# Another PSUM pool for the state product, attention stages one slot sooner, and a higher rank for some VectorE operations

## The chip, the cores and the metric

The kernel runs on one core of a Trainium2 chip. The metric is the time of one execution on the device in microseconds (us), from the first to the last instruction with what lies around them; less is better. The engines are TensorE (PE in the rows, with its weight loads as PEld), VectorE (DVE), ScalarE (ACT), GpSimd (POOL) and the DMA queues, most of them issued by SyncE (SP). Each engine works through its own instructions in order and waits on semaphores for the others.

## The reference

Linear attention with a decaying state, then two feed-forward layers on its output. There are 4 batches, 8 heads, 768 tokens and 48 features per head; the first layer is 384 to 2048 to 384, the second 384 to 1024 to 384.

```python
for t in range(S):                      # attention, per batch and head
    cur = einsum('bhd,bhe->bhde', u * k_t, v_t)
    y_t = einsum('bhd,bhde->bhe', r_t, state + cur)
    state = w_t[..., None] * state + einsum('bhd,bhe->bhde', k_t, v_t)
x = y as tokens x (heads * features)    # 3072 x 384
h = x @ w_in
x = (h * clip(h + 3, 0, 6) / 6) @ w_out
h = x @ w_in2
h = h * softmax(h);  h = layernorm(h) * g_ln
out = h @ w_out2
```

## The kernel before

**Attention.** The sequence is cut into 6 groups of 128 tokens; with 4 batches that makes 24 tiles, numbered i = 4 * group + batch. For a tile the decay of the state is a product along the tokens, so that the tile becomes matmuls. Its stages are `stw` (GpSimd clips w into wc), `st0` (TensorE transposes wc to wt and r to rt; VectorE scans wt backward into q, L500, four scans, takes a reciprocal and scans wt forward into e, L506, four scans; then e = rt * e, L510), `st1` (TensorE transposes k to kt; VectorE q = kt * q, L524; GpSimd z = r * k, then z * u, L526 and L527), `st2` (a transpose ktp of q, read by ScalarE; VectorE sums z into d, L561; TensorE pa = e * q in two halves; GpSimd makes the diagonal block am from d, L572, for each half; VectorE copies the strictly causal part of pa over it, L576) and `st3` (TensorE kv, the product that goes into the state, L585, and yt, the output, L600 and L607; VectorE adds kv to the decayed state, L626; ScalarE rounds yt to xh and VectorE makes the rest xl, L639). Tiles from 10 on get their transposes in another way; L626, L639 and st2 are the same there.

**First layer.** A group's four tiles give 512 tokens, and its weights are used in 16 slots n: `ffn_in(n)` makes h in 9 matmuls (high and low parts of x and of the weights), ScalarE, VectorE (L662, t) and ScalarE again make gh from it, GpSimd makes the rest gl, and `ffn_out(n - 2)` adds 9 matmuls into y. The slots of group 0 run while the attention of tiles 4 to 8 does. The weights of the first slots also come in at that time, packed, and are decoded by ScalarE (L63, L71) and VectorE: L66, L50, L53 and L72 on 128 x 768 elements, once each for a slot, from buffers `raw` that are loaded again when L53 has read them.

**PSUM.** `ps_a` has three banks, which wt, rt, kt, ktp, the two halves pa, kv and yt take in turn; a tile that takes a bank waits until the last reader of the one before is done. `ps_h` has two, for h. y has three of its own. kv of the tiles up to 8 is in `ps_a`, later in `ps_h`:

```python
kv = ps_tile("kv") if i < JOIN - 1 else ps_h.tile([P, HP, P], F32, tag="h", name="kv")
```

**Order.** A table gives each stage of each tile a slot, 4 slots for a tile, and `back` moves a stage ahead of the slot (negative) or behind it:

```python
back = 2 if s == NS - 1 else s - 3 if i < JOIN else s - 5
sched.setdefault(4 * (i - B) + back, []).append((i, s))
```

On TensorE, VectorE, ScalarE and GpSimd a scheduler then sets the order by priority, which follows the program's order unless something raises it; SyncE keeps the program's order.

Of the kernel before, what the change touches and what calls it, by code (L numbers as in the profile page):

```python
# [8 lines left out]
F32 = mybir.dt.float32  # L9
# [4 lines left out]
ALU = mybir.AluOpType  # L14
# [4 lines left out]
P = 128  # L19
# [259 lines left out]
def fast_path(  # L279
# [14 lines left out]
    nc = tc.nc  # L294
# [4 lines left out]
    C = P  # L299
# [157 lines left out]
    def stw(i):  # L457
# [25 lines left out]
            out=junk, in_=a["w"][:, :, 0:D], func=ACTF.Relu, bias=b_hi, accum_out=chk[:, 3 * i + 1:3 * i + 2]  # L483
        )

    def st0(i):
        a = at[i]
        g = i // B
        if i < LATE:
            wt = ps_in(i, "wt", "y0")  # L490
            trans(wt, a["wc"])
            rt = ps_in(i, "rt", "y1")
            trans(rt, a["r"])
        else:
            wt, rt = flip("w"), flip("r")
        q = atp.tile([P, HP, C + 1], F32, tag="q", name="q")
        e = atp.tile([P, HP, C], F32, tag="e", name="e")
        nc.gpsimd.memset(q[0:DP, :, C:C + 1], 1.0)
        for hp in range(HP):
            nc.vector.tensor_tensor_scan(  # L500
                out=q[0:DP, hp, 0:C][:, ::-1], data0=wt[0:DP, hp, :][:, ::-1], data1=ones[0:DP, :],
                initial=1.0, op0=ALU.mult, op1=ALU.mult,
            )
        nc.vector.reciprocal(out=e[0:DP, :, 0], in_=q[0:DP, :, 0])
        for hp in range(HP):
            nc.vector.tensor_tensor_scan(  # L506
                out=e[0:DP, hp, 1:C], data0=wt[0:DP, hp, 0:C - 1], data1=ones[0:DP, 0:C - 1],
                initial=e[0:DP, hp, 0:1], op0=ALU.mult, op1=ALU.mult,
            )
        nc.vector.tensor_tensor(out=e[0:DP], in0=rt[0:DP], in1=e[0:DP], op=ALU.mult)  # L510
        a.update(q=q, e=e)

    def st1(i):
        a = at[i]
        g, b = divmod(i, B)
        q = a["q"]
        if i < LATE:
            kt = ps_in(i, "kt", "y2")
            trans(kt, a["k"])
        else:  # L520
            kt = flip("k")
        if 0 < g and i < JOIN:
            state_in(i)
        nc.vector.tensor_tensor(out=q[0:DP, :, 1:C + 1], in0=kt[0:DP], in1=q[0:DP, :, 1:C + 1], op=ALU.mult)  # L524
        z = a["r"][:, :, 0:D]
        nc.gpsimd.tensor_tensor(out=z, in0=z, in1=a["k"][:, :, 0:D], op=ALU.mult)  # L526
        nc.gpsimd.tensor_tensor(out=z, in0=z, in1=u_bc, op=ALU.mult)  # L527
        a["z"] = z
# [17 lines left out]
    def st2(i):  # L546
        a = at[i]
        g = i // B
        kq = a["q"][:, :, 1:C + 1]
        rr = a["e"]  # L550
        if g < NG - 1:
            ktp = ps_tile("ktp")
            for hp in range(HP):
                nc.tensor.transpose(out=ktp[:, hp, 0:DP], in_=kq[0:DP, hp, :], identity=ident[0:DP, 0:DP])
            ktok = atp.tile([P, HP, DP], F32, tag="ktok", name="ktok")
            nc.scalar.activation(out=ktok, in_=ktp[:, :, 0:DP], func=ACTF.Copy)
            a["ktok"] = ktok
        a["am"] = []
        pas = [ps_tile("pa0"), ps_tile("pa1")]
        d = atp.tile([P, H], F32, tag="d", name="d")  # L560
        nc.vector.tensor_reduce(out=d, in_=a["z"], axis=AX.X, op=ALU.add)  # L561
        for j in range(HP):
            for hh, pa in enumerate(pas):
                o = 64 * hh
                nc.tensor.matmul(
                    out=pa[:, j, :], lhsT=kq[o:o + D, j, :], rhs=rr[o:o + D, j, :], start=True, stop=True
                )
        dv = d.rearrange("p (j hh) -> p hh j", hh=2)
        for hh, pa in enumerate(pas):
            am = atp.tile([P, 4, C], F32, tag="am", name="am")  # L570
            a["am"].append(am)
            nc.gpsimd.tensor_tensor(  # L572
                out=am, in0=ident.unsqueeze(1).to_broadcast([P, HP, C]),
                in1=dv[:, hh, :].unsqueeze(2).to_broadcast([P, HP, C]), op=ALU.mult,
            )
            nc.vector.copy_predicated(am, causal.unsqueeze(1).to_broadcast([P, HP, C]), pa)  # L576

    def st3(i):
        a = at[i]
        g, b = divmod(i, B)  # L580
        if g < NG - 1:
            kv = ps_tile("kv") if i < JOIN - 1 else ps_h.tile([P, HP, P], F32, tag="h", name="kv")
            for h in range(H):
                o = 64 * (h % 2)
                nc.tensor.matmul(  # L585
                    out=kv[o:o + D, h // 2, 0:D], lhsT=a["ktok"][:, h // 2, o:o + D], rhs=a["v"][:, h, :],
                    start=True, stop=True, skip_group_check=True,
                )
# [31 lines left out]
        if g < NG - 1:  # L620
            for j in range(2):
                o, f = 64 * j, D * j
                dst = s_st[b][o:o + D, :, f:f + D]
                src = kv[o:o + D, :, 0:D]
                if g > 0:
                    nc.vector.tensor_tensor(out=dst, in0=src, in1=a["sp"][o:o + D, :, f:f + D], op=ALU.add)  # L626
                else:
                    nc.scalar.activation(out=dst, in_=src, func=ACTF.Copy)
        at.pop(i)
# [6 lines left out]
        sl = slice(b * C, (b + 1) * C)  # L636
        xf = y[:, 0:KD, :]
        nc.scalar.activation(out=xh[:, :, sl], in_=xf, func=ACTF.Copy, accum_out=chk[:, 3 * i + 2:3 * i + 3])
        nc.vector.tensor_tensor(out=xl[:, :, sl], in0=xf, in1=xh[:, :, sl].bitcast(F32), op=ALU.subtract)  # L639

    stages = [stw, st0, st1, st2, st3]

# [160 lines left out]
    sched = {}  # L803
    for i in range(B, NTILE):
        for s in range(NS):
            back = 2 if s == NS - 1 else s - 3 if i < JOIN else s - 5
            sched.setdefault(4 * (i - B) + back, []).append((i, s))
    for n in sorted(q for q in sched if q < 0):
        for i, s in sched[n]:
# [5 lines left out]
    for n in range(NSLOT + LAG):  # L815
        if n < NSLOT:
            ffn_in(n)
        for i, s in sorted(sched.get(n, []), key=lambda x: (x[0] - 2 * (x[0] >= JOIN and x[1] == 3), x[1])):
            stages[s](i)
            if s == NS - 1 and JOIN <= i + 1 < NTILE:  # L820
                state_in(i + 1)
            if s == 3:
                load_to(i + 3)
            if s == (0 if i + 1 == LATE else 2) and LATE <= i + 1 < NTILE:
                load_late(i + 1)
        if n >= LAG:
            ffn_out(n - LAG)
        if n + LD < M1:
            w1_b(n + LD)
        if n + LD + 1 < M1:  # L830
            w1_a(n + LD + 1)
        if n + LD + 3 < M1:
            w1_load(n + LD + 3)
        if n == M1:
            dec_st.close()
            late_open()
        if n == NA:
            row = range_a()
            right.close()
            w2_open()  # L840
            w2_load(0)
            w2_load(1)
        j = n - NA
        if 1 <= j <= 2 * M2:
            w2_b(j - 1)
        if 0 <= j < 2 * M2:
            w2_a(j)
        if 1 <= j <= 2 * M2 - 2:
            w2_load(j + 1)
# [115 lines left out]
```

## Time and profile before

| | |
|---|---|
| three runs | 781.13 us median (779.6, 781.13, 781.53) |
| the profiled execution | 780.79 us |
| its span, first to last instruction | 779.1 us |
| mean granted clock of TensorE | 0.976 |
| TensorE busy | 736.6 us (95%) |
| VectorE busy | 531.6 us (68%) |
| ScalarE busy | 333.6 us (43%) |
| GpSimd busy | 262.0 us (34%) |

The profiled execution lasts 1.7 us longer than its span, and lies within the three runs. A share of busy time is a mean over stages that differ: the stretch in which the weights of the first layer are decoded, up to about 143 us, is read by itself. A granted clock of 1 is TensorE's upper level, 2.4 GHz, and 0.5 is 1.2 GHz.

### The profile page before, as it was taken

To read this page: it belongs to the slowest core of one execution; us is meant where nothing else is said; L and a number is where in the kernel's file an instruction comes from. 1 tells how busy PE (TensorE), PEld (TensorE's weight loads), DVE (VectorE), ACT (ScalarE), POOL (GpSimd) and SP (SyncE) were. 2 spreads that over 40 slices of the span, in tenths; PEclk is the share of its full clock that TensorE was granted. 3 is DMA by queue.
4 is the path that set the end of the run, shared out by engine and by line. 5 is a ranking of instruction groups with operands and counts; after the bars stand their busy time and mean duration, and the time that the engine had idled before them with its cause. 6 is when DMAs were issued, how large, how long until landed. Compare 5 with 4: busy or idle time off the path is not lost. (4 is left out here: it accounts for less than half of the span.)

```text
span 779.1 us, 13589 instructions
## 1 busy us (share of the span) xinstructions
PE 736.6 (95%) x5084; PEld 621.3 (80%) x5084; DVE 531.6 (68%) x1010; ACT 333.6 (43%) x647; POOL 262.0 (34%) x355
## 2 busy tenths in 40 slices
PE   6669798999999999999999999999999999999996
PEld 4547676888888888888888887877889999999996
DVE  6989889667677777777778856886565555555552
ACT  3455555334444334433344335654444344333442
POOL 5566647642333233333233211232222222222200
PEclk8889997999999999999999999999999999999999
DMA  9785653514345333433334003440111111111001
GB/s 172 176 167 138 163 131 97 108 41 86 84 85 126 84 84 85 125 85 85 85 89 120 1 1 104 145 133 26 61 42 42 51 41 41 48 45 42 31 20 36
DMA packets 139435, 64.79 MB, mean 83 GB/s; under 512 B 90848, under 2 KB 133984, under 8 KB 139360
## 3 DMA queue, kind: packets, MB, share of 16 engines
q1 hardware_dynamic: 136768, 59.11, 32.2%
q10 hardware_dynamic: 2592, 4.72, 1.6%
q8 instruction: 42, 0.69, 0.4%
q14 instruction: 33, 0.27, 0.1%
HBM read 54.37 MB, written 9.44 MB: 82 GB/s over the span
## 5 line engine op out<-in xcount | busy, mean ns | idle before, releaser
L677 PE MATMUL y<-gh,w_h 128*128 128x512 f32 x288 | 116.7, 405 | 1.0 <-ACT ye L683 1.0
L657 PE MATMUL h<-xh,w_h 128*128 128x512 f32 x288 | 113.0, 393 | 3.0 <-DVE t L662 2.9
L677 PE MATMUL y<-gl,w_h 128*128 128x512 f32 x288 | 114.0, 396 | 0.0
L677 PE MATMUL y<-gh,w_l 128*128 128x512 f32 x288 | 113.4, 394 | 0.0
L657 PE MATMUL h<-xl,w_h 128*128 128x512 f32 x288 | 112.8, 392 | 0.0
L657 PE MATMUL h<-xh,w_l 128*128 128x512 f32 x288 | 112.5, 391 | 0.0
L661 ACT ACTIVATE t<-h,cols 128x512 f32<-128x512 f32 x96 | 65.3, 681 | 104.9 <-PE h L657 101.8
L663 ACT ACTIVATE gh<-t 128x512 fp32r<-128x512 f32 x96 | 60.5, 630 | 103.7 <-DVE t L662 103.5
L662 DVE SCALAR_TENSOR_TENSOR t<-t,h 128x512 f32<-128x512 f32 x96 | 65.4, 681 | 41.2 <-ACT t L661 41.0
L665 DVE TENSOR_TENSOR gl<-t,gh 128x512 fp32r<-128x512 f32 x80 | 66.8, 835 | 36.0 <-ACT gh L663 35.0
L78 DVE TENSOR_REDUCE nm<-h 128x1 f32<-128x1024 f32 x24 | 29.4, 1226 | 61.5 <-PE h L872 61.4
L899 PE MATMUL po<-w_oh,qh 128*128 128x384 f32 x192 | 67.1, 350 | 0.3 <-ACT qh L888 0.3
L657 PEld LDWEIGHTS h<-xh,w_h 128*128 128x128 f32 x288 | 54.4, 189 | 16.0 <-DVE t L662 4.2
L677 PEld LDWEIGHTS y<-gh,w_h 128*128 128x128 f32 x288 | 54.7, 190 | 15.5 <-issue 3.2
L899 PE MATMUL po<-w_oh,ql 128*128 128x384 f32 x192 | 64.7, 337 | 0.1
L899 PE MATMUL po<-w_ol,qh 128*128 128x384 f32 x192 | 64.8, 337 | 0.0
L677 PEld LDWEIGHTS y<-gh,w_l 128*128 128x128 f32 x288 | 54.9, 191 | 11.8
L677 PEld LDWEIGHTS y<-gl,w_h 128*128 128x128 f32 x288 | 55.0, 191 | 11.0 <-DVE gl L665 0.6
L657 PEld LDWEIGHTS h<-xh,w_l 128*128 128x128 f32 x288 | 54.4, 189 | 11.3
L657 PEld LDWEIGHTS h<-xl,w_h 128*128 128x128 f32 x288 | 54.4, 189 | 11.2
L888 ACT ACTIVATE qh<-pt 128x512 fp32r<-128x512 f32 x48 | 26.1, 597 | 78.3 <-PE pt L886 78.3
L872 PE MATMUL h<-w_ih,yl 128*128 128x512 f32 x144 | 56.4, 391 | 0.0
(123 smaller groups left out, 1478.7 us busy)
## 6 DMA issues: line engine op xcount, KB each, us to landing
raw<-in_moe_w_out_dram SPq DMA_DIRECT2D x24, 384.0 KB, 5.9
raw<-in_moe_w_in_dram SPq DMA_DIRECT2D x48, 128.0 KB
r<-in_r_dram SPq DMA_DIRECT2D x24, 192.0 KB
k<-in_k_dram SPq DMA_DIRECT2D x24, 192.0 KB, 3.7
v<-in_v_dram SPq DMA_DIRECT2D x24, 192.0 KB, 4.0
y1d<-ye ACTq DMA_DIRECT2D x18, 256.0 KB, 2.3
y<-y1d SPq DMA_DIRECT2D x24, 192.0 KB, 2.8
out_dram<-os SPq DMA_DIRECT2D x24, 192.0 KB, 1.9
```

What stands on the lines that cost most here:

```text
L78: nc.vector.tensor_reduce(out=nm, in_=h, axis=AX.X, op=ALU.max, negate=True)
L657: nc.tensor.matmul(out=h, lhsT=a, rhs=b, start=(j == 0), stop=(j == len(ops) - 1))
L661: nc.scalar.activation(out=t, in_=h, func=ACTF.Relu, bias=three)
L662: nc.vector.scalar_tensor_tensor(out=t, in0=t, scalar=6.0, in1=h, op0=ALU.min, op1=ALU.mult)
L663: nc.scalar.activation(out=gh, in_=t, func=ACTF.Copy)
L665: eng.tensor_tensor(out=gl, in0=t, in1=gh.bitcast(F32), op=ALU.subtract)
L677: nc.tensor.matmul(out=y_ps[g][c], lhsT=a, rhs=b, start=(m == 0 and j == 0), stop=(m == M1 - 1 and j == 2))
L872: nc.tensor.matmul(out=h[:, fs], lhsT=a[:, c, :], rhs=b_[:, c, fs], start=(j == 0), stop=(j == len(ops) - 1))
L888: nc.scalar.activation(out=qh[:, ms, :], in_=pt, func=ACTF.Copy)
L899: nc.tensor.matmul(out=po, lhsT=x[:, m, :], rhs=y[:, m, :], start=(n == 0), stop=(n == 3 * M2 - 1))
```

## The change

It adds and removes no instruction. The state product kv of the tiles from 4 on goes into the h pair, so that `ps_a` has seven takers for a tile instead of eight. For tiles 5 to 9 `stw`, `st0` and `st1` come one slot sooner (`back` of -4, -3, -2 instead of -3, -2, -1); `st2` and `st3` stay. The VectorE operations of L510, L524, L576, L626 and L639 of tiles 4 to 9 get a raised priority. One load of tile 10 is issued with another stage, in the same slot.

```diff
--- before.py
+++ after.py
@@ -483,6 +483,9 @@
             out=junk, in_=a["w"][:, :, 0:D], func=ACTF.Relu, bias=b_hi, accum_out=chk[:, 3 * i + 1:3 * i + 2]
         )
 
+    def early(i):
+        return tc.high_priority() if B <= i < JOIN else ExitStack()
+
     def st0(i):
         a = at[i]
         g = i // B
@@ -507,7 +510,8 @@
                 out=e[0:DP, hp, 1:C], data0=wt[0:DP, hp, 0:C - 1], data1=ones[0:DP, 0:C - 1],
                 initial=e[0:DP, hp, 0:1], op0=ALU.mult, op1=ALU.mult,
             )
-        nc.vector.tensor_tensor(out=e[0:DP], in0=rt[0:DP], in1=e[0:DP], op=ALU.mult)
+        with early(i):
+            nc.vector.tensor_tensor(out=e[0:DP], in0=rt[0:DP], in1=e[0:DP], op=ALU.mult)
         a.update(q=q, e=e)
 
     def st1(i):
@@ -521,7 +525,8 @@
             kt = flip("k")
         if 0 < g and i < JOIN:
             state_in(i)
-        nc.vector.tensor_tensor(out=q[0:DP, :, 1:C + 1], in0=kt[0:DP], in1=q[0:DP, :, 1:C + 1], op=ALU.mult)
+        with early(i):
+            nc.vector.tensor_tensor(out=q[0:DP, :, 1:C + 1], in0=kt[0:DP], in1=q[0:DP, :, 1:C + 1], op=ALU.mult)
         z = a["r"][:, :, 0:D]
         nc.gpsimd.tensor_tensor(out=z, in0=z, in1=a["k"][:, :, 0:D], op=ALU.mult)
         nc.gpsimd.tensor_tensor(out=z, in0=z, in1=u_bc, op=ALU.mult)
@@ -573,13 +578,14 @@
                 out=am, in0=ident.unsqueeze(1).to_broadcast([P, HP, C]),
                 in1=dv[:, hh, :].unsqueeze(2).to_broadcast([P, HP, C]), op=ALU.mult,
             )
-            nc.vector.copy_predicated(am, causal.unsqueeze(1).to_broadcast([P, HP, C]), pa)
+            with early(i):
+                nc.vector.copy_predicated(am, causal.unsqueeze(1).to_broadcast([P, HP, C]), pa)
 
     def st3(i):
         a = at[i]
         g, b = divmod(i, B)
         if g < NG - 1:
-            kv = ps_tile("kv") if i < JOIN - 1 else ps_h.tile([P, HP, P], F32, tag="h", name="kv")
+            kv = ps_tile("kv") if i < B else ps_h.tile([P, HP, P], F32, tag="h", name="kv")
             for h in range(H):
                 o = 64 * (h % 2)
                 nc.tensor.matmul(
@@ -623,7 +629,8 @@
                 dst = s_st[b][o:o + D, :, f:f + D]
                 src = kv[o:o + D, :, 0:D]
                 if g > 0:
-                    nc.vector.tensor_tensor(out=dst, in0=src, in1=a["sp"][o:o + D, :, f:f + D], op=ALU.add)
+                    with early(i):
+                        nc.vector.tensor_tensor(out=dst, in0=src, in1=a["sp"][o:o + D, :, f:f + D], op=ALU.add)
                 else:
                     nc.scalar.activation(out=dst, in_=src, func=ACTF.Copy)
         at.pop(i)
@@ -636,7 +643,8 @@
         sl = slice(b * C, (b + 1) * C)
         xf = y[:, 0:KD, :]
         nc.scalar.activation(out=xh[:, :, sl], in_=xf, func=ACTF.Copy, accum_out=chk[:, 3 * i + 2:3 * i + 3])
-        nc.vector.tensor_tensor(out=xl[:, :, sl], in0=xf, in1=xh[:, :, sl].bitcast(F32), op=ALU.subtract)
+        with early(i):
+            nc.vector.tensor_tensor(out=xl[:, :, sl], in0=xf, in1=xh[:, :, sl].bitcast(F32), op=ALU.subtract)
 
     stages = [stw, st0, st1, st2, st3]
 
@@ -803,7 +811,7 @@
     sched = {}
     for i in range(B, NTILE):
         for s in range(NS):
-            back = 2 if s == NS - 1 else s - 3 if i < JOIN else s - 5
+            back = 2 if s == NS - 1 else (-4, -3, -2, 0)[s] if i < JOIN else s - 5
             sched.setdefault(4 * (i - B) + back, []).append((i, s))
     for n in sorted(q for q in sched if q < 0):
         for i, s in sched[n]:
@@ -821,7 +829,7 @@
                 state_in(i + 1)
             if s == 3:
                 load_to(i + 3)
-            if s == (0 if i + 1 == LATE else 2) and LATE <= i + 1 < NTILE:
+            if s == (1 if i + 1 == LATE else 2) and LATE <= i + 1 < NTILE:
                 load_late(i + 1)
         if n >= LAG:
             ffn_out(n - LAG)
```

The lines of the code move by 3 to 8 (L576 of before is L582 of the change, L626 is L633, L662 is L670, L677 is L685, and so on).

The first place is TensorE between tiles 5 and 6. In before the transposes wt and rt of tile 6 stand behind yt of tile 5, rt among the y matmuls of a slot; `y_836` to `y_838` are the three y banks. Before:

```order
L600 MATMUL yt<-e,sr 32x128 x4
L455 MATMUL wt<-ident,wc 112x128 x4
L677 MATMUL y_836<-gh,w_h 128x512
L677 MATMUL y_836<-gl,w_h 128x512
L677 MATMUL y_836<-gh,w_l 128x512
L677 MATMUL y_837<-gh,w_h 128x512
L677 MATMUL y_837<-gl,w_h 128x512
L677 MATMUL y_837<-gh,w_l 128x512
L677 MATMUL y_838<-gh,w_h 128x512
L455 MATMUL rt<-ident,r 112x128 x4
```

In the change (its y banks are `y_848` to `y_850`) wt and rt of tile 6 stand two slots of matmuls ahead of that:

```order
L665 MATMUL h<-xl,w_h 128x512
L665 MATMUL h<-xh,w_l 128x512
L455 MATMUL wt<-ident,wc 112x128 x4
L455 MATMUL rt<-ident,r 112x128 x4
L685 MATMUL y_848<-gh,w_h 128x512
L685 MATMUL y_848<-gl,w_h 128x512
```

and behind yt of tile 5 stands kt of tile 6:

```order
L606 MATMUL yt<-e,sr 32x128 x4
L685 MATMUL y_848<-gh,w_h 128x512
L685 MATMUL y_848<-gl,w_h 128x512
L685 MATMUL y_848<-gh,w_l 128x512
L685 MATMUL y_849<-gh,w_h 128x512
L685 MATMUL y_849<-gl,w_h 128x512
L685 MATMUL y_849<-gh,w_l 128x512
L685 MATMUL y_850<-gh,w_h 128x512
L455 MATMUL kt<-ident,k 112x128 x4
```

So rt of tile 6 moved ahead of kv and yt of tile 5, and kt has taken about the place that rt had.

The second place is VectorE, from the second mask copy of tile 5 on (`pa_934` and `pa_935` are the two halves of pa). Before:

```order
L576 COPY_PREDICATED am<-causal,pa_935 128x512
L50 SCALAR_TENSOR_TENSOR dec<-dec,raw 128x768
L66 TENSOR_SCALAR raw<-raw 128x768
L53 SCALAR_TENSOR_TENSOR dec<-raw,dec 128x768
L662 SCALAR_TENSOR_TENSOR t<-t,h 128x512
L50 SCALAR_TENSOR_TENSOR dec<-dec,raw 128x768
L72 TENSOR_TENSOR w_l<-dec,w_h 128x768
L53 SCALAR_TENSOR_TENSOR dec<-raw,dec 128x768
L662 SCALAR_TENSOR_TENSOR t<-t,h 128x512
L66 TENSOR_SCALAR raw<-raw 128x768
L72 TENSOR_TENSOR w_l<-dec,w_h 128x768
L626 TENSOR_TENSOR s_st_115<-kv,sp 48x4x48 x2
```

In the change:

```order
L582 COPY_PREDICATED am<-causal,pa_935 128x512
L72 TENSOR_TENSOR w_l<-dec,w_h 128x768
L53 SCALAR_TENSOR_TENSOR dec<-raw,dec 128x768
L670 SCALAR_TENSOR_TENSOR t<-t,h 128x512
L66 TENSOR_SCALAR raw<-raw 128x768
L72 TENSOR_TENSOR w_l<-dec,w_h 128x768
L503 SCALAR_TENSOR_TENSOR q<-wt,ones 112x128 x4
L50 SCALAR_TENSOR_TENSOR dec<-dec,raw 128x768
L633 TENSOR_TENSOR s_st_115<-kv,sp 48x4x48 x2
L507 RECIPROCAL e<-q 112x4
L53 SCALAR_TENSOR_TENSOR dec<-raw,dec 128x768
```

The q scans of tile 6 and the add of kv now come with fewer decode operations ahead of them: an L50 went ahead of the mask copies, an L72, an L53 and their like are in another order, and the q scans moved ahead of the state's add.

The third place is TensorE behind yt of tile 7, before:

```order
L607 MATMUL yt<-am,v 16x128 x4
L600 MATMUL yt<-e,sr 32x128 x4
L455 MATMUL wt<-ident,wc 112x128 x4
L455 MATMUL rt<-ident,r 112x128 x4
L677 MATMUL y_836<-gh,w_h 128x512
L677 MATMUL y_836<-gl,w_h 128x512
```

and in the change, where wt and rt of tile 8 stand a slot sooner, and kt of tile 8 is what follows:

```order
L613 MATMUL yt<-am,v 16x128 x4
L606 MATMUL yt<-e,sr 32x128 x4
L455 MATMUL kt<-ident,k 112x128 x4
L685 MATMUL y_848<-gh,w_h 128x512
L685 MATMUL y_848<-gl,w_h 128x512
```

On VectorE the change has these operations from the last mask copy of tile 7 to the e scans of tile 8:

```order
L582 COPY_PREDICATED am<-causal,pa_1465 128x512
L72 TENSOR_TENSOR w_l<-dec,w_h 128x768
L670 SCALAR_TENSOR_TENSOR t<-t,h 128x512
L53 SCALAR_TENSOR_TENSOR dec<-raw,dec 128x768
L503 SCALAR_TENSOR_TENSOR q<-wt,ones 112x128 x2
L670 SCALAR_TENSOR_TENSOR t<-t,h 128x512
L72 TENSOR_TENSOR w_l<-dec,w_h 128x768
L503 SCALAR_TENSOR_TENSOR q<-wt,ones 112x128 x2
L566 TENSOR_REDUCE d<-r 128x8
L507 RECIPROCAL e<-q 112x4
L509 SCALAR_TENSOR_TENSOR e<-wt,e,ones 112x127 x4
```

In before kt of tile 8 stood a slot later, and the scans had the same place behind the last mask copy, with the adds of tile 7's state (L626) ahead of them.

## Rows read from the trace of the kernel before

**Rows 1.** The page: TensorE's busy share in 40 slices and its granted clock.

```profile
PE   6669798999999999999999999999999999999996
...
PEclk8889997999999999999999999999999999999999
```

**Rows 2.** Timeline of TensorE: start, length, instruction, idle time before it and releaser.

```profile
75.55 0.60 PE L554 MATMUL ktp<-ident,q 112*128 112x112 f32 x4 [0.98 <-DVE q L524]
...
93.20 0.84 PE L455 MATMUL rt<-ident,r 128*112 128x128 f32 x4 [4.56 <-issue]
...
117.75 0.86 PE L455 MATMUL rt<-ident,r 128*112 128x128 f32 x3 [2.26 <-issue]
...
131.13 1.01 PE L554 MATMUL ktp<-ident,q 112*128 112x112 f32 x4 [2.67 <-DVE q L524]
```

**Rows 3.** Windows: TensorE, its weight loads, VectorE, ScalarE, GpSimd busy; clock; DMA share.

```profile
57.28:142.87 85.59, 74.03 (x546) 59.24 (x543) 75.76 (x118) 44.53 (x86) 50.03 (x47) 0.92 0.53 127
93.20:97.00 3.80, 3.80 (x12) 3.12 (x13) 2.89 (x8) 1.01 (x2) 3.34 (x5) 0.55 0.56 181
117.70:121.00 3.30, 3.25 (x10) 2.76 (x11) 3.27 (x5) 1.90 (x5) 3.06 (x4) 0.53 0.72 205
131.10:137.60 6.50, 6.47 (x28) 5.26 (x29) 4.86 (x7) 2.88 (x6) 6.50 (x5) 0.50 0.35 61
```

**Rows 4.** Waits of VectorE from 57.2 to 142.9: total, times, longest.

```profile
DVE am L576 <- POOL am L572: 7.3, 6, 1.5
```

**Rows 5.** Lines of VectorE from 57.2 to 142.9: busy, mean ns, idle before.

```profile
L53 DVE SCALAR_TENSOR_TENSOR dec<-raw,dec 128x768 int32<-128x768 int32 x13 | 13.5, 1041 | 0.0
L50 DVE SCALAR_TENSOR_TENSOR dec<-dec,raw 128x768 int32<-128x768 int32 x12 | 13.3, 1106 | 0.0
L72 DVE TENSOR_TENSOR w_l<-dec,w_h 128x768 fp32r<-128x768 f32 x13 | 12.9, 993 | 1.1 <-ACT w_h L71 1.1
L662 DVE SCALAR_TENSOR_TENSOR t<-t,h 128x512 f32<-128x512 f32 x14 | 9.5, 678 | 0.1
L66 DVE TENSOR_SCALAR raw<-raw 128x768 int32<-128x768 int32 x12 | 8.9, 740 | 1.1 <-ACT dec L63 1.1
...
L506 DVE TENSOR_TENSOR_SCAN e<-wt,e,ones 112x127 f32<-112x127 f32 x12 | 4.8, 455 | 0.0
L500 DVE TENSOR_TENSOR_SCAN q<-wt,ones 112x128 f32<-112x128 f32 x12 | 4.1, 402 | 0.0
```

**Rows 6.** Timeline of VectorE, six places.

```profile
58.62 1.39 DVE L576 COPY_PREDICATED am<-causal,pa 128x512 f32<-128x512 int32 x2
...
84.82 0.57 DVE L66 TENSOR_SCALAR raw<-raw 128x768 int32<-128x768 int32 x1
85.29 0.95 DVE L53 SCALAR_TENSOR_TENSOR dec<-raw,dec 128x768 int32<-128x768 int32 x1
...
88.49 2.03 DVE L53 SCALAR_TENSOR_TENSOR dec<-raw,dec 128x768 int32<-128x768 int32 x1
...
92.39 0.71 DVE L626 TENSOR_TENSOR s_st<-kv,sp 48x192 f32<-48x192 f32 x2
...
138.41 0.75 DVE L576 COPY_PREDICATED am<-causal,pa 128x512 f32<-128x512 int32 x1 [1.51 <-POOL am L572]
```

**Rows 7.** Timeline of GpSimd (POOL), three places.

```profile
87.72 1.99 POOL L665 TENSOR_TENSOR gl<-t,gh 128x512 fp32r<-128x512 f32 x1 [4.28 <-ACT gh L663]
...
94.12 1.01 POOL L526 TENSOR_TENSOR r<-r,k 128x384 f32<-128x384 f32 x1 [0.38 <-PE rt L455]
...
109.83 1.04 POOL L572 TENSOR_TENSOR am<-ident,d 128x512 f32<-128x512 f32 x1
```

**Rows 8.** Timelines of TensorE and of VectorE at tile 8.

```profile
146.89 0.60 PE L455 MATMUL rt<-ident,r 128*112 128x128 f32 x4
147.25 0.47 PE L677 MATMUL y<-gh,w_h 128*128 128x512 f32 x1
...
150.85 0.55 DVE L561 TENSOR_REDUCE d<-r 128x8 f32<-128x384 f32 x1 [1.93 <-POOL r L527]
```

## The prediction

> **What bounds the kernel now.** The page's slices come first [rows 1]: TensorE is full and at its upper clock level (2.4 GHz) from the eighth slice on, that is from about 136 us. Only the start, where attention tiles 4 to 8 run, has holes. The timeline of TensorE shows these [rows 2]: gaps of 0.98, 4.56, 2.26 and 2.67 us, together 10.5, before ktp of tile 5, rt of 6, rt of 7 and ktp of 7 (others are shorter). After the three larger ones the windows give a granted clock of 0.55, 0.53 and 0.50 (the level of 1.2 GHz) for 3.80, 3.30 and 6.50 us [rows 3], which loses 3.80 x 0.45 + 3.30 x 0.47 + 6.50 x 0.50 = 6.5 us. So about 17 us is the most that a start without these gaps could give.
>
> The profile puts two of these gaps down to "issue". The real releaser stands in VectorE's timeline: L626 starts at 92.39 and lasts 0.71, ends at 93.10, and rt of tile 6 starts at 93.20. It reads kv, whose bank rt takes over. The change aims at this wait. But who is late: TensorE, or VectorE? VectorE is busy 75.76 of the 85.59 us of this stretch [rows 3], and the list of its waits says for what it is idle [rows 4]: 7.3 us for GpSimd's diagonal blocks (L572); the lines add 1.1 of L66 and 1.1 of L72 for ScalarE's halves of the decode [rows 5]. TensorE isn't there. As long as VectorE never waits for TensorE, TensorE's gaps are slack: filling one makes TensorE wait elsewhere. Only from 142 us, when the decode of weights has ended, does VectorE wait for TensorE.
>
> VectorE loses more than its idle time. In the lines [rows 5] L50, L53, L72 and L66 mean 1106, 1041, 993 and 740 ns; rows with nothing beside them take 0.95 (L53 at 85.29) and 0.57 (L66 at 84.82) [rows 6], and I take 0.95 for the other two operations on 128x768, too. The excess is 12 x 0.16 + 13 x 0.09 + 13 x 0.04 + 12 x 0.17 = 5.7 us. Its cause shows in one pair: L53 at 88.49 takes 2.03 where GpSimd's gl runs from 87.72 to 89.71 [rows 6, 7]; 89.71 plus a step of 0.87 is 90.58, its end is 90.52. The VectorE operation stands still until GpSimd's ends. (The Trainium skill, "SBUF — State Buffer", section "Who interferes with whom", says that the two share a pair of ports under a lock held for a whole instruction, and that a VectorE operation with two SBUF inputs takes it; the trace agrees with that here, 2.03 us against 0.95.)
>
> **The change part by part.** No instruction is added or removed; the profiled 780.79 us (span 779.1) is the base, 0.34 under the runs' median of 781.13.
>
> *kv in the h pair; wt, rt and kt one slot sooner.* rt(i+1) then waits for tile i's last mask copy, not for L626, and the gap of 4.56 as it stood is gone. In exchange kt(i+1) stands right behind tile i's yt and waits for VectorE's xl (tiles 5, 6), or for the e scans of its own tile, with whose wt it shares a bank (tiles 7, 8, 9). Also kv takes an h buffer, so that the next h waits for L626. TensorE's work is the same; its waits change place, and what decides is when VectorE gets through.
>
> *Rank.* L510, L524, L576, L626 and L639 go ahead of decode operations. VectorE's busy time stays; only the order changes. The decode ends behind instead, which costs nothing while VectorE's total is what counts.
>
> *GpSimd.* r x k (1.01 us alone [rows 7]) and r x u of tile i+1 can start right behind the mask copies, since rt comes sooner; there VectorE does L72, L53, L66, which stand still beside them.
>
> So the term to price is VectorE's loss from the end of tile 4's last mask copy to that of tile 7's. In before these ends are 59.9 (two copies from 58.62, steps of 0.64: a row less the 0.1 by which it overlaps the next) and 139.05 (138.41 + 0.64) [rows 6], 79.1 us apart, of which 9.5 is idle and 6.6 lost at the ports (by steps from start to start; 5.7 of it are the lengthened rows above): 16.1. For after, I laid the new order of VectorE against GpSimd's, with the step lengths above: L50, L53, L72 at 0.87, L66 at 0.47, t at 0.60, and where a decode operation meets a GpSimd operation, the rest of that one is added. For tile 6: L72 beside r x k 0.55, L66 beside r x u 0.45, L50, L50 and L66 beside gl 0.65 each, the last L50 beside gl 0.80: 3.75. The diagonal blocks then cost 1.35 (1.0 ahead of the first, as L50 runs while GpSimd works; 0.35 for the second, since both blocks now stand together on GpSimd, 1.04 each [rows 7] against a copy of 0.64). In before this was 7.3 over three tiles [rows 4], 2.4 for each. Tile 6 loses 5.1, tile 7 4.6 and tile 5 5.6 (a raw load comes later, as its buffer's last reader L53 does). Sum 15.3, thus waits 16.1 - 15.3 = **0.8 us** better: 9.5 to 4.05 in idle time, 6.6 to 11.25 at the ports.
>
> *Where it meets TensorE.* The first place at which TensorE is what counts is kt of tile 8. In before the y block behind rt of tile 8 starts at 147.25, 0.36 after rt [rows 8]; a kt of 0.36 more is still owed, so 147.6 is the equal point. In after kt's bank is free when the e scans of tile 8 are done: from the last mask copy's end, VectorE has L72, t, L53, two q scans, t, L72, two q scans (0.87 + 0.60 + 0.87 + 0.64 + 0.60 + 0.87 + 0.64 = 5.1), then d, which waits for r x u behind gl and wc on GpSimd (1.75 of waits there and at the ports, an estimate from the order), then 0.47 for d and 1.6 for the reciprocal and four e scans (0.08 taken off the means [rows 5, 8], as above), then kt 0.36: 9.3 in all. The last copy ends at 139.05 - 0.8, and L72 and t (1.47) have moved behind it while an L50 (0.87) moved ahead, another 0.6; the walk, unrounded, has 137.5. kt ends at 146.8, 0.8 before the equal point. From there TensorE sets the pace in both kernels with the same work. 780.79 - 0.8 = **780.0 us**. The unknown: the new wait at kt of tile 8, and so whether the clock falls there. It may be 1.3 to 3.4 us, by how late TensorE comes. In before the gap of 2.26 was followed by the lower level [rows 2, 3].
>
> Bounds of the port term, which no row of before prices in the new order: from below the mean of before, 5.7 us over the three tiles; from above the walk's 11.25. I take the upper, as operations that lose their lock move toward GpSimd's, as the pair at 88.49 shows. (The page named above speaks against the change here: by its rule each new meeting of L72 or L53 with r x k costs the rest of it; by the mean of before the sum would be 774.5.)
>
> **The rivals.** *Faster.* The new meetings don't happen, since GpSimd's operations, too, stand still and shift into VectorE's reads from PSUM (t, scans, copies), which are not lengthened. Then ports cost 5.7 rather than 11.25 us, 5.5 better: 780.0 - 5.5 = 774.5. For it: L53, at a mean of 1041 against 950, mostly escaped in before; VectorE's idle time of 9.5 does shrink by the order. Against: GpSimd stood idle for 4.28 us ahead of gl at 87.72 [rows 7], waiting for gh; such idle time is where operations escaped, and r x k and r x u now fill some of it. TensorE's gaps, gone altogether, would give 17 (764 us); that is out, since VectorE alone needs its busy 75.76 in this stretch.
>
> *Slower.* kt of tile 8 stood free of VectorE in before and now waits for the scans. If VectorE gains nothing, kt ends at 139.05 + 9.3 = 148.35, 0.8 late, and TensorE goes on at 0.50 as it did behind 131.13, which loses 3.25: 780.79 + 4.0 = 784.8. It decides where TensorE's wait there passes some 2.3 us. For it: d of tile 8 waited 1.93 for r x u in before, too [rows 8], hidden there. Against: VectorE's idle time for diagonal blocks must then stay at 7.3.
>
> That the change doesn't move what it says is excluded: the order shows wt and rt ahead and kv out of the rotation.
>
> **How the numbers follow.** What tells from no change is about 0.3%, 2.3 us. VectorE sets the pace, 778.5 to 782.5: 0.42. Faster, centred on 774.5: 0.38. Slower, at 783.2 to 785: 0.20. The range of 773.5 to 784.0 leaves out the ends of both rivals. The cases give faster 0.38, same 0.42, slower 0.20.
>
> **What would show it.** Right: rt of tile 6 starts without the 4.56, and waits of 2 to 4 us stand before kt of tiles 6 to 8 instead; VectorE's idle time for L572 falls from 7.3 to about 4; the means of L72, L53 and L66 rise over 993, 1041 and 740; tile 7's last mask copy ends at 137.5; y behind kt of tile 8 starts at 146.8. Wrong, if those means fall or stay while the copy ends by 134 (the faster rival), or if the copy ends near 139 and the clock falls behind kt of tile 8 (the slower one). The prediction also falls if VectorE is found waiting for TensorE in the stretch before 142 us: then the gaps were not slack.

## The result and the profile after

The changed kernel takes 785.53 us (median of 6 runs, 782.82 to 786.05), the one before 781.52 us in the same runs. The ratio is 1.0055, with a 95% interval of 1.0041 to 1.0069: about 4.3 us slower (the medians differ by 4.0). The profiled execution takes 785.19 us (span 783.5), 4.4 more than before's 780.79.

On the page, TensorE and its clock in 40 slices:

```profile
PE   5669889899999999999999999999999999999996
...
PEclk9888899999999999999999999999999999999999
```

The start is filled differently from [rows 1], and the last hole now lies in the eighth slice, where before had none. The timeline of TensorE has the gaps (start, length, instruction, idle time before it and what ended it):

```profile
57.45 0.50 PE L665 MATMUL h<-xh,w_h 128*128 128x512 f32 x1 [2.71 <-DVE t L670]
...
87.21 1.10 PE L455 MATMUL rt<-ident,r 128*112 128x128 f32 x4 [3.89 <-DVE am L582]
...
114.90 0.65 PE L455 MATMUL rt<-ident,r 128*112 128x128 f32 x4 [2.93 <-DVE am L582]
...
125.28 0.62 PE L455 MATMUL kt<-ident,k 128*112 128x128 f32 x4 [1.18 <-issue]
...
150.65 0.65 PE L455 MATMUL kt<-ident,k 128*112 128x128 f32 x2 [3.08 <-issue]
```

The gap of 4.56 ahead of rt of tile 6 [rows 2] has become 3.89, ended by tile 5's mask copy; a gap of 2.93 stands ahead of rt of tile 7, one of 1.18 ahead of kt of tile 7; a gap ahead of kt of tile 8 is new, 3.08, and a window (TensorE, its weight loads, VectorE, ScalarE and GpSimd busy; clock) shows the lower level, 0.53, behind it:

```profile
150.60:154.00 3.40, 3.35 (x11) 2.86 (x12) 2.74 (x6) 1.27 (x4) 1.85 (x3) 0.53 0.69 168
```

VectorE's timeline says where the lateness is from. First from tile 4's product on, then the second mask copies of tiles 5 and 6, then tiles 7 and 8:

```profile
51.54 0.68 DVE L529 TENSOR_TENSOR q<-kt,q 112x512 f32<-112x512 f32 x1
52.13 0.17 DVE L507 RECIPROCAL e<-q 112x4 f32<-112x4 f32 x1
52.22 3.08 DVE L50 SCALAR_TENSOR_TENSOR dec<-dec,raw 128x768 int32<-128x768 int32 x1
55.23 1.59 DVE L509 TENSOR_TENSOR_SCAN e<-wt,e,ones 112x127 f32<-112x127 f32 x4
...
60.59 1.36 DVE L582 COPY_PREDICATED am<-causal,pa 128x512 f32<-128x512 int32 x2 [0.66 <-PE pa L570]
61.85 1.18 DVE L72 TENSOR_TENSOR w_l<-dec,w_h 128x768 fp32r<-128x768 f32 x1
...
65.54 0.72 DVE L633 TENSOR_TENSOR s_st<-kv,sp 48x192 f32<-48x192 f32 x2 [1.55 <-PE kv L591]
...
87.43 0.73 DVE L582 COPY_PREDICATED am<-causal,pa 128x512 f32<-128x512 int32 x1 [0.27 <-POOL am L577]
...
115.12 0.75 DVE L582 COPY_PREDICATED am<-causal,pa 128x512 f32<-128x512 int32 x1 [0.27 <-POOL am L577]
115.75 1.72 DVE L53 SCALAR_TENSOR_TENSOR dec<-raw,dec 128x768 int32<-128x768 int32 x1
117.40 1.38 DVE L66 TENSOR_SCALAR raw<-raw 128x768 int32<-128x768 int32 x1
...
139.87 1.33 DVE L582 COPY_PREDICATED am<-causal,pa 128x512 f32<-128x512 int32 x2
...
148.27 0.55 DVE L566 TENSOR_REDUCE d<-r 128x8 f32<-128x384 f32 x1 [2.02 <-POOL r L532]
...
148.95 1.60 DVE L509 TENSOR_TENSOR_SCAN e<-wt,e,ones 112x127 f32<-112x127 f32 x4
```

L50 at 52.22 takes 3.08 us, and the e scans stand behind it. GpSimd's timeline beside it:

```profile
51.94 0.40 POOL L544 TENSOR_TENSOR sr<-s_st,q 112x128 f32<-112x128 f32 x1
...
52.45 2.04 POOL L577 TENSOR_TENSOR am<-ident,d 128x512 f32<-128x512 f32 x2
```

L50 came while GpSimd's sr ran, and stood still through both diagonal blocks, up to 54.49; 54.49 and a step of 0.87 make 55.36, its end is 55.30. In before, VectorE's timeline has the scans ahead, and an L50 behind them took 1.59:

```profile
52.48 0.66 DVE L524 TENSOR_TENSOR q<-kt,q 112x512 f32<-112x512 f32 x1
53.06 1.59 DVE L506 TENSOR_TENSOR_SCAN e<-wt,e,ones 112x127 f32<-112x127 f32 x4
54.57 1.59 DVE L50 SCALAR_TENSOR_TENSOR dec<-dec,raw 128x768 int32<-128x768 int32 x1
```

So in the change e of tile 4, the halves pa and the mask copies come late, and TensorE waits 2.71 us at 57.45 for t (L670), which VectorE has behind the scans.

The lines of VectorE (busy, mean ns, idle before) from 57.2 to 142 us, and its waits from 61.8 to 142:

```profile
L72 DVE TENSOR_TENSOR w_l<-dec,w_h 128x768 fp32r<-128x768 f32 x12 | 14.1, 1178 | 0.1
L50 DVE SCALAR_TENSOR_TENSOR dec<-dec,raw 128x768 int32<-128x768 int32 x12 | 14.1, 1175 | 0.0
L53 DVE SCALAR_TENSOR_TENSOR dec<-raw,dec 128x768 int32<-128x768 int32 x12 | 14.1, 1172 | 0.0
L66 DVE TENSOR_SCALAR raw<-raw 128x768 int32<-128x768 int32 x12 | 9.5, 792 | 0.8 <-ACT dec L63 0.8
```

```profile
DVE am L582 <- POOL am L577: 2.4, 4, 0.9
DVE s_st L633 <- PE kv L591: 1.6, 1, 1.6
```

The four means have risen over those of [rows 5]; idle time for diagonal blocks fell from 7.3 [rows 4] to 2.4; and a wait of VectorE for TensorE is there, 1.6 us, for kv of tile 4 (at 65.54).

### The profile page after: what moved, and what is told of

It is laid out like the page before. It is cut to its first block, busy times and chain, and to the rows that moved or that the text cites. A ratio compares the mean times of both kernels' runs of the same rounds, so it can differ in the third digit from the quotient of the medians.

```text
span 783.5 us, 13597 instructions
## 1 busy us (share of the span) xinstructions
PE 738.6 (94%) x5084; PEld 622.6 (79%) x5084; DVE 541.6 (69%) x1010; ACT 334.0 (43%) x647; POOL 260.7 (33%) x355
## 5 line engine op out<-in xcount | busy, mean ns | idle before, releaser
L685 PE MATMUL y<-gh,w_h 128*128 128x512 f32 x288 | 117.1, 406 | 0.7 <-ACT ye L691 0.7
L685 PE MATMUL y<-gl,w_h 128*128 128x512 f32 x288 | 114.4, 397 | 0.3 <-DVE gl L673 0.3
L685 PE MATMUL y<-gh,w_l 128*128 128x512 f32 x288 | 113.8, 395 | 0.0
L670 DVE SCALAR_TENSOR_TENSOR t<-t,h 128x512 f32<-128x512 f32 x96 | 65.4, 682 | 44.3 <-ACT t L669 44.1
L673 DVE TENSOR_TENSOR gl<-t,gh 128x512 fp32r<-128x512 f32 x80 | 69.6, 870 | 35.8 <-ACT gh L671 34.8
L685 PEld LDWEIGHTS y<-gh,w_h 128*128 128x128 f32 x288 | 55.0, 191 | 15.9 <-issue 3.6
L685 PEld LDWEIGHTS y<-gh,w_l 128*128 128x128 f32 x288 | 55.1, 191 | 11.8
L685 PEld LDWEIGHTS y<-gl,w_h 128*128 128x128 f32 x288 | 55.0, 191 | 11.4 <-DVE gl L673 1.1
```

Source lines behind the costliest of these rows:

```text
L670: nc.vector.scalar_tensor_tensor(out=t, in0=t, scalar=6.0, in1=h, op0=ALU.min, op1=ALU.mult)
L673: eng.tensor_tensor(out=gl, in0=t, in1=gh.bitcast(F32), op=ALU.subtract)
L685: nc.tensor.matmul(out=y_ps[g][c], lhsT=a, rhs=b, start=(m == 0 and j == 0), stop=(m == M1 - 1 and j == 2))
```

## The experiments

All were timed in five rounds against the kernel before on the same chip. The table has them all, by the trace of each: from the start of the first yt of tile 3 that is done under its mask (at 44.9 to 46.4 us) to the end of tile 4's last mask copy; from there to tile 7's last; from there to the end of the span. Since a decode operation stands ahead of a copy in one kernel and behind it in another, and since each row is one execution, the sections are to be read to about 1 us: up to tile 4's copies e10 runs the same instructions as the change, and the two differ by 1.2 there.

| kernel | to tile 4's copies | tiles 5 to 7 | to the end | ratio to before, of all runs (95%) |
|---|---|---|---|---|
| before | 14.36 | 79.15 | 640.0 | 1 |
| the change | 16.97 | 79.25 | 642.4 | 1.0055 (1.0041 to 1.0069) |
| e1, no rank in tile 4 | 14.65 | 78.46 | 642.8 | 1.0017 (1.0004 to 1.0030) |
| e2, no rank | 14.24 | 80.30 | 640.7 | 1.0008 (0.9995 to 1.0020) |
| e3, kv alone | 14.75 | 80.77 | 639.7 | 1.0019 (1.0007 to 1.0031) |
| e4, rank alone | 16.98 | 81.51 | 638.0 | 1.0038 (1.0025 to 1.0051) |
| e5, scans in the rank | 14.18 | 75.62 | 641.9 | 0.9994 (0.9983 to 1.0005) |
| e6, no rank, w early | 14.56 | 86.46 | 639.0 | 1.0098 (1.0081 to 1.0116) |
| e7, before, w early | 14.75 | 80.02 | 639.5 | 1.0000 (0.9988 to 1.0011) |
| e8, e1 with tiles 5 to 7 sooner | 14.73 | 78.16 | 638.3 | 0.9973 (0.9961 to 0.9985) |
| e9, e5 with tiles 5 to 7 sooner | 14.55 | 76.29 | 637.8 | 0.9935 (0.9916 to 0.9953) |
| e10, change, small u | 18.16 | 77.69 | 641.9 | 1.0036 (1.0020 to 1.0052) |
| e11, before, small u | 14.16 | 79.58 | 639.5 | 0.9989 (0.9975 to 1.0002) |
| e12, e2 with tiles 5 to 7 sooner | 14.74 | 79.38 | 636.8 | 0.9987 (0.9975 to 0.9998) |

**e1: the change without tile 4's rank.**

```diff
-        return tc.high_priority() if B <= i < JOIN else ExitStack()
+        return tc.high_priority() if B < i < JOIN else ExitStack()
```

> The change with the raised rank for tiles 5 to 9 only. Theory A (the time is lost where tile 4's rank puts an L50 ahead of its e scans: that L50 took 3.08 us, VectorE then came 2.0 us late to tile 4's mask copies, and TensorE waited 2.71 for t): the e scans stand ahead of L50 again, VectorE leaves tile 4's copies near 59.9 instead of 61.85, and the time falls by 2 to 3.5 us against the change, to 782.0 to 783.5. Theory B (the loss is GpSimd's r x k and r x u meeting the decode at the shared port, in all tiles): the start moves, but the time stays at 785 to 786. Theory C (kt of tile 8 waits for the e scans, 3.08 us in the change, whatever comes before): a wait of about 3 us stays in front of kt of tile 8, and the time stays over 784.

Measured: 781.89 us, ratio 1.0017 where the change has 1.0055: 0.38% or 3.0 us less. Theory A holds for this part: tile 4's copies come 14.65 us behind the start, as in before. Of theory C the wait came, the same ahead of kt of tile 8 (timeline of TensorE), but not the time, which was to stay over 784:

```profile
148.87 0.62 PE L455 MATMUL kt<-ident,k 128*112 128x128 f32 x4 [3.08 <-issue]
```

**e2: the change without any rank.**

```diff
-        return tc.high_priority() if B <= i < JOIN else ExitStack()
+        return tc.high_priority() if False else ExitStack()
```

> The change without any raised rank: kv in the h pair and the stages one slot sooner alone. Theory A: no L50 ahead of tile 4's e scans, so 782 to 783.5 as without tile 4's rank; if the rank of tiles 5 to 8 does what it is for, some tenths to 1 us more than that. Theory B: 785 to 786, since r x k and r x u meet the decode all the same. Theory C: the wait ahead of kt of tile 8 stays near 3 us and the time over 784.

Measured: 781.42 us, 1.0008, not to be told from e1, and under the 782 at which theory A's range began: the rank of tiles 5 to 9 as the change has it gains nothing that can be seen here. In this trace tiles 5 to 7 take longer, for a reason that nothing had named. ScalarE's timeline, and VectorE's behind it:

```profile
128.74 0.62 ACT L479 ACTIVATE junk<-w,cols 128x384 bf16<-128x384 f32 x1 [4.20 <-DMA w<-in_w_dram]
...
129.35 0.83 ACT L71 ACTIVATE w_h<-dec 128x768 fp32r<-128x768 f32 x1
```

```profile
126.49 0.95 DVE L50 SCALAR_TENSOR_TENSOR dec<-dec,raw 128x768 int32<-128x768 int32 x1
130.22 0.96 DVE L72 TENSOR_TENSOR w_l<-dec,w_h 128x768 fp32r<-128x768 f32 x1 [2.78 <-ACT w_h L71]
```

ScalarE's range check of tile 9 (it is the tenth L479 of the timeline; the expectations of e6, e7 and e12 call it tile 8's) comes a slot sooner and waits 4.20 us for a load that doesn't; the decode's w_h is queued behind it, and VectorE's L72 waits 2.78 for that.

The wait ahead of kt of tile 8, on the other hand, is not there, although tile 8 is as much ahead as in the change (TensorE's timeline, then GpSimd's in e2, then GpSimd's in the change):

```profile
148.02 0.65 PE L455 MATMUL kt<-ident,k 128*112 128x128 f32 x4
```

```profile
141.53 1.03 POOL L532 TENSOR_TENSOR r<-r,u_bc 128x384 f32<-128x384 f32 x1
143.13 1.58 POOL L673 TENSOR_TENSOR gl<-t,gh 128x512 fp32r<-128x512 f32 x1 [0.57 <-ACT gh L671]
```

```profile
143.38 1.30 POOL L673 TENSOR_TENSOR gl<-t,gh 128x512 fp32r<-128x512 f32 x1 [4.11 <-ACT gh L671]
...
147.24 0.99 POOL L532 TENSOR_TENSOR r<-r,u_bc 128x384 f32<-128x384 f32 x1
```

Without rank GpSimd has r x u of tile 8 ahead of gl, so d and the e scans are done in time. In the change, gl stands ahead of it and waits 4.11 us for ScalarE's gh. So the earlier slot makes kt of tile 8 wait only together with the order that the rank brings; e2 has a gap of 3.07 ahead of rt of tile 8 instead.

**e3: kv alone.**

```diff
-            kv = ps_tile("kv") if i < JOIN - 1 else ps_h.tile([P, HP, P], F32, tag="h", name="kv")
+            kv = ps_tile("kv") if i < B else ps_h.tile([P, HP, P], F32, tag="h", name="kv")
```

> The kernel before with kv of tiles 4 to 8 in the h pair, nothing else. If VectorE sets the pace up to 142 us, TensorE's waits move and the time is that of before within 1 us, 780.5 to 782.5. If TensorE's gaps were the bound, the gaps of 4.56 and 2.26 ahead of rt go and the time falls to 776 to 778. If kv in the h pair costs by itself (the next h waits for L626), it rises to 783 or more.

Measured: 782.23 us, 1.0019: within the first case, at its upper end. The gaps ahead of rt are gone, and those ahead of ktp have grown in their place, as TensorE's timeline has it, against 0.98 and 2.67 for tiles 5 and 7 in before [rows 2]:

```profile
77.32 0.60 PE L554 MATMUL ktp<-ident,q 112*128 112x112 f32 x4 [2.33 <-DVE q L524]
...
104.72 0.60 PE L554 MATMUL ktp<-ident,q 112*128 112x112 f32 x4 [3.69 <-DVE q L524]
...
133.63 0.63 PE L554 MATMUL ktp<-ident,q 112*128 112x112 f32 x2 [4.23 <-DVE q L524]
```

TensorE's gaps there were slack, as the prediction had it. Why the time is 0.19% longer than before's isn't settled.

**e4: rank alone**, the change with two lines of before (the load of tile 10 as in before, too):

```diff
-            back = 2 if s == NS - 1 else (-4, -3, -2, 0)[s] if i < JOIN else s - 5
+            back = 2 if s == NS - 1 else s - 3 if i < JOIN else s - 5
-            kv = ps_tile("kv") if i < B else ...
+            kv = ps_tile("kv") if i < JOIN - 1 else ...
```

> The kernel before with the raised rank alone. The same L50 stands ahead of tile 4's e scans as in the change. Theory A: tile 4's mask copies come about 2 us late and the time rises by 1.5 to 2.5 us over before, to 783 to 784. Theory B: r x k and r x u stay where they were, so 781 to 782.

Measured: 783.59 us, 1.0038, theory A's forecast. An L50 of 3.08 us stands ahead of the e scans here, too, and tile 4's copies come 16.98 us behind the start.

**e5: the scans in the rank.**

```diff
-        nc.vector.reciprocal(out=e[0:DP, :, 0], in_=q[0:DP, :, 0])
-        for hp in range(HP):
-            nc.vector.tensor_tensor_scan(
 ...
+        with early(i):
+            nc.vector.reciprocal(out=e[0:DP, :, 0], in_=q[0:DP, :, 0])
+            for hp in range(HP):
+                nc.vector.tensor_tensor_scan(
 ...
```

> The change with the reciprocal and the e scans in the raised rank, too, so that in tile 4 no L50 stands between q = kt * q and the e scans. Theory A (what tile 4's rank costs is that L50 ahead of unraised scans): as with tile 4 left out of the rank, 782 or less, 3 us or more under the change. Rival (raising L510, L524 or L576 of tile 4 costs by itself, whatever stands ahead of the scans): 784.5 to 786.

Measured: 779.19 us where before had 780.14, ratio 0.9994, 4.8 us (0.61%) under the change. Tile 4's rank costs nothing if the scans have it, too (14.18 us to its copies): it was the hole in the chain. Which of the raised operations lets the L50 in, no run tells. The rest of the 4.8 us lies in tiles 5 to 7, whose scans are raised as well. VectorE is done with tile 7's copies at 135.05, 4 us sooner than in before, and the kernel isn't faster, as kt of tile 8 waits all the same:

```profile
144.60 0.65 PE L455 MATMUL kt<-ident,k 128*112 128x128 f32 x2 [3.35 <-issue]
```

**e6 and e7: the load of w earlier.** Without rank (e6), and in the kernel before (e7). load_w, which is new, loads w of one tile alone, and the load of the whole tile then leaves w out (not shown); the call is:

```diff
+            if s == 2 and B < i < LATE - 2:
+                load_w(i + 2)
```

> The change without rank, with the load of w for tiles 7 to 9 issued with stage 1 of the tile two before (two slots sooner) instead of with its stage 2. Without rank ScalarE's range check of tile 8 waited 4.20 us for that load, and VectorE 2.78 us behind it for the decode's w_h. Theory D (the stages one slot sooner wait for a load that is not sooner, and that eats the gain): the two waits go and the time falls by 2 to 3 us, to 778 to 779.5. Rival (VectorE makes up for it, or TensorE sets the pace by then): 781 to 782.

> The kernel before with the same earlier load of w and nothing else. There the check of tile 8 waited 3.33 us for the load. Theory D: VectorE was hit by less than 1 us of it in before, so the time is that of before to 1 us less, 779.7 to 781. Rival (the load alone is worth as much in either): 778 to 779.

Measured: e6 787.76 us, 1.0098, against every expectation; e7 1.0000, within theory D's. In e6 the checks of tiles 7 and 8 went ahead about as much as their loads (against e2, 9.9 and 6.7 us for 9.1 and 5.5), and the load of tile 9 came later: ScalarE's three waits for w (timeline) are 3.59, 2.18 and 3.75 us,

```profile
76.40 0.61 ACT L488 ACTIVATE junk<-w,cols 128x384 bf16<-128x384 f32 x1 [3.59 <-DMA w<-in_w_dram]
...
106.31 0.62 ACT L488 ACTIVATE junk<-w,cols 128x384 bf16<-128x384 f32 x1 [2.18 <-DMA w<-in_w_dram]
...
136.35 0.61 ACT L488 ACTIVATE junk<-w,cols 128x384 bf16<-128x384 f32 x1 [3.75 <-DMA w<-in_w_dram]
```

and tiles 5 to 7 take 86.46 us, 6.2 more than in e2. VectorE waits 6.2 us for ScalarE's w_h there, 2.8 in e2, and 6.1 for diagonal blocks, 3.6 in e2, which is most of it. In e7 the checks wait for w, too: 4.62 for tile 9, where before has 3.33, and 8.8 in all, where before has 3.7; but VectorE waits only 0.3 for w_h. So the edit took the waits away in neither kernel, and theory D stays untested.

**e8: e1 with tiles 8 and 9 on their old slots** (and the load of tile 10 as in before).

```diff
-            back = 2 if s == NS - 1 else (-4, -3, -2, 0)[s] if i < JOIN else s - 5
+            back = 2 if s == NS - 1 else (-4, -3, -2, 0)[s] if i < 8 else s - 3 if i < JOIN else s - 5
-            if s == (1 if i + 1 == LATE else 2) and LATE <= i + 1 < NTILE:
+            if s == (0 if i + 1 == LATE else 2) and LATE <= i + 1 < NTILE:
```

> The change with rank for tiles 5 to 9 only and the stages one slot sooner for tiles 5 to 7 only, so that kt of tile 8 stands a slot behind its rt again. Theory C (kt of tile 8, 3.08 us behind the e scans, and the lower clock behind it cost what tiles 6 and 7 gained): no wait ahead of kt of tile 8 and 1 to 2.5 us under the run without tile 4's rank, 779.5 to 781. Rival (another wait of TensorE for VectorE takes its place at rt of tile 8): 781.5 to 782.5.

Measured: 778.14 us where before had 780.14, ratio 0.9973, 0.44% or 3.4 us under e1. More than was expected; no wait stands ahead of kt of tile 8, the clock stays at 1.00 from 138.5 to 152 (window),

```profile
138.50:152.00 13.50, 12.26 (x122) 9.84 (x121) 9.69 (x20) 6.78 (x13) 9.65 (x16) 1.00 0.35 82
```

and the section to the end is 4.5 us shorter in these two executions.

**e9: both remedies.** The edit of e5 and the one shown for e8 together.

> The change with the reciprocal and e scans in the raised rank and the stages one slot sooner for tiles 5 to 7 only: the two remedies together. If they add, 2.5 to 3 us under the run with the raised scans alone, 775.5 to 777.5, with no wait ahead of kt of tile 8. Rival (both take away the same microseconds, as VectorE's total sets the pace from tile 5 on): 778 to 779, as with tiles 5 to 7 sooner alone.

Measured: 775.73 us where before had 780.89, ratio 0.9935 (0.9916 to 0.9953): 5.1 us faster than the kernel before and 9.4 us (1.2%) faster than the change. The two add up. Beside e8, which leaves out tile 4's rank altogether, e9 gains another 0.38%, 3.0 us: the raised scans help in tiles 5 to 7, too (76.29 for 78.16), and don't only close tile 4's hole.

**e10 and e11: a smaller z * u on GpSimd**, in the change and in before. The factor u is left out for seven of the eight heads of tiles 5 to 9, so the two compute something else:

```diff
-        nc.gpsimd.tensor_tensor(out=z, in0=z, in1=u_bc, op=ALU.mult)
+        zu, uu = (z[:, 0:1, :], u_bc[:, 0:1, :]) if B < i < LATE else (z, u_bc)
+        nc.gpsimd.tensor_tensor(out=zu, in0=zu, in1=uu, op=ALU.mult)
```

> The change with GpSimd's z * u of tiles 5 to 9 cut to one of 8 heads (the factor u is left out for the other heads of these tiles); the order of every engine stays. Theory B (GpSimd's operations that now meet the decode hold VectorE up): L66 beside it falls from 1.38 to 0.55, d of tile 8 comes about 0.9 sooner, and the time falls by 2.5 to 4 us, to 781.5 to 783. Rival (these meetings are off the path, as TensorE or ScalarE is what VectorE waits for): within 1 us of the change.

> The kernel before with the same cut of z * u for tiles 5 to 9. Theory B: before meets r x u with L66 too, but its TensorE takes over at 142 us, so that 0 to 2 us are gained, 778.5 to 780.5, less than in the change. Rival: no change in either.

Measured: 1.0036, 0.19% or 1.5 us under the change, and 0.9989, 0.9 us under before. That lies between theory B and its rival, and by the intervals neither step is clear of noise (1.5 us, give or take 1.7), so the two runs don't decide. In the trace of e10 d of tile 8 comes 0.7 us sooner than in the change (147.58 for 148.27), where theory B had 0.9. VectorE's timeline behind tile 6's copies, and GpSimd's:

```profile
116.22 0.95 DVE L53 SCALAR_TENSOR_TENSOR dec<-raw,dec 128x768 int32<-128x768 int32 x1
117.08 1.41 DVE L66 TENSOR_SCALAR raw<-raw 128x768 int32<-128x768 int32 x1
```

```profile
116.34 1.73 POOL L531 TENSOR_TENSOR r<-r,k 128x384 f32<-128x384 f32 x1 [0.63 <-PE rt L455]
118.14 0.49 POOL L533 TENSOR_TENSOR r<-r,u_bc 128x48 f32<-128x48 f32 x1
```

L53 started first here, and r x k stood still until it was done (1.73, ended at 118.07); then L66 stood still for r x k, 1.41. In the change r x k was first, L53 took 1.72, and L66 met r x u (1.38). So about a tenth of a microsecond decides who waits for whom, and the operation that is cut isn't the only one that L66 can meet.

**e12: no rank, tiles 5 to 7 sooner.** The edit of e2 and the one shown for e8.

> The change without any raised rank, and with the stages one slot sooner for tiles 5 to 7 only. Without rank and with tiles 8 and 9 sooner, ScalarE's range check of tile 8 waited 4.20 us for its load and VectorE 2.78 us behind it. If tile 8 being sooner is what costs there, too, that wait shrinks and the time is 2 to 3 us under the run without rank, 778 to 779.5. If the raised rank with the scans is what makes the best version, this one stays 2 us or more over it, and if rank is worth nothing it comes to 775 to 776.5.

Measured: 779.53 us, 0.9987, 0.21% under e2, about half of what the same edit gives in e8 (in e2 there was no wait ahead of kt of tile 8 to take away). It stays 0.5% or 4 us over e9: the rank is worth that much, once it takes in the scans and tile 8 is left alone.

## Why the prediction was wrong

**The step that failed** is "So the term to price is VectorE's loss from the end of tile 4's last mask copy", with the same start, 59.9, in both. The part on rank said "VectorE's busy time stays; only the order changes", and the order was looked at from tile 5 on. In tile 4 the rank raised q = kt * q over the reciprocal, and an L50 came in between, ahead of the unraised scans: 2.6 us from yt of tile 3 to tile 4's copies (16.97 against 14.36). e4 shows that cost with the rank alone, e1 and e5 show that it goes when tile 4's rank goes or the hole in it is closed.

**Its signs** came only in part. rt of tile 6 does start without the 4.56 and the means rise; but the waits of 3.89 and 2.93 stand ahead of rt of tiles 6 and 7, and of kt only tile 8's waits 2 to 4 us (3.08; tile 7's 1.18). Tile 7's last copy ended at 141.1, not 137.5.

**kt's end of tile 8** was forecast for 146.8. It started at 150.65 and would have ended at 151.0 with the 0.36 of [rows 8] (at the lower level y behind it starts at 151.37). Of these 4.2 us, 1.95 are the start of the stretch (61.85 for 59.9), 1.65 the stretch (79.25 for 137.5 - 59.9 = 77.6), 0.6 the tail behind the last copy (9.9 for 9.3).

**The stretch** itself was right in its two parts. The port term was 11.25; the means of the four lines over the prediction's 0.95 and 0.57 give 12 x 0.23 (L72) + 12 x 0.22 (L50) + 12 x 0.22 (L53) + 12 x 0.22 (L66) = 10.7. (Counted this way before has 5.7; the 11.25 is to be held against 6.6, so the rise is 5.0 where 4.65 was forecast.) Idle time for diagonal blocks was forecast to be about 4 and is 2.4. Two things were missing. One is L697, a small operation that stood behind tile 7's last copy in before and now stands ahead of it, and takes 1.01 us. The other is VectorE's wait of 1.55 us for kv of tile 4 at 65.54. The prediction said "As long as VectorE never waits for TensorE", and named this as what would make it fall; TensorE was late there, as it had waited 2.71 for t at 57.45. In e1 0.3 of that wait is left, in e5 nothing.

**The mechanism of the slower rival** was the right one: kt of tile 8 waits for the scans, the wait passes 2.3 us (3.08), and the clock falls behind it in the change, in e1 and in e5. But 2.3 is no limit that decides this, as the last section shows. Its sizes were off, too: it had kt 0.8 late and 3.25 for the clock; it is 3.4 late against the equal point of 147.6, and 3.4 us at 0.53 lose 1.6. Together 5.0, where the spans differ by 4.4; the remaining 0.6 I haven't followed. That its 784.8 came so near to 785.5 is luck, then, since it knew nothing of tile 4. Its point against ("VectorE's idle time for diagonal blocks must then stay at 7.3") was no condition: the idle time fell, and kt was late for another reason. e8 and e9 show that the stages of tiles 8 and 9 cost 3.4 and 4.6 us by standing one slot sooner under the raised rank (d of tile 8 waits 2.02 for r x u at 148.27, which stands behind gl on GpSimd, then the scans come; in e2, without rank, neither wait is there), and e5 that this eats even a gain of 4 us on VectorE.

**The faster rival** had 6.3 us, and 5.1 are there (e9), but only with the scans in the rank and tiles 8 and 9 as they were. It doesn't come from fewer losses at the port: in e9 L50, L72, L53 and L66 still mean 1206, 1195, 1066 and 760 ns, none under before. What is less is VectorE's idle time from tile 4's copies to tile 7's, 2.4 us where before has 9.5.

**Rightly forecast**: the gaps of TensorE ahead of rt were slack (e3), and the three parts of the change together could not give 17 us.

What stays open: why tiles 5 to 7 take 3.5 us less in e5 than in before. VectorE waits 2.7 us for diagonal blocks where before has 7.3, and not at all for ScalarE where before has 2.2; the ports take back a part of that, and no run took it apart.

## What to carry to other kernels

Raise a whole chain or nothing: an operation that is left out of the raised rank in the middle of a chain lets unrelated work in ahead of it, and if that work shares a port with a neighbour, the hole costs 3 us where the work alone takes 1. Where a stage is moved ahead for several tiles, look at the last of them by itself, where another engine takes over the pace: here the move cost 3 to 5 us there under the raised rank. And a walk through the order has to begin where the first instruction changes its place, not where the loop of interest begins.

## What the hardware showed that was not expected

An operation on 128 x 16 elements (L697, 0.18 us in before) takes 1.01 in the change, where GpSimd's second diagonal block of tile 7 runs beside it. VectorE's row and GpSimd's (timelines):

```profile
138.08 1.01 DVE L697 TENSOR_SCALAR chk<-chk 128x16 f32<-128x16 f32 x1
```

```profile
137.70 1.36 POOL L577 TENSOR_TENSOR am<-ident,d 128x512 f32<-128x512 f32 x1
```

GpSimd's ends at 139.06, VectorE's at 139.09: the small operation paid what was left of the other one. In e12, where it has no such neighbour, it takes 0.17. And the clock fell behind the gap ahead of kt of tile 8 in e5, too, where TensorE's timeline shows no other gap from 119.87 on: a stretch without a gap, at 1.00 from 130 to 141 us, didn't keep it up behind 3.35 us (0.59 from 144.5 to 148).

The length of a gap alone doesn't tell whether the clock falls behind it. In TensorE's timeline of e1 these two gaps were followed by 1.00 (windows from 113 to 116 and from 123.5 to 127):

```profile
113.13 0.65 PE L455 MATMUL rt<-ident,r 128*112 128x128 f32 x4 [2.87 <-DVE am L582]
...
123.50 0.62 PE L455 MATMUL kt<-ident,k 128*112 128x128 f32 x4 [2.76 <-issue]
```

Ahead of rt of tile 7, before has 2.26 and 0.53 behind it [rows 2, 3], e11 2.28 and 1.00 behind it (117.6 to 121). So whether such a gap costs the lower clock can't be forecast from its length, and the prediction's limit of 2.3 us came from one case.
